# A fused attention and MLP kernel on one core: wider unread matmuls at the start, 256-column cuts, and products in two halves

## The chip, the core and the metric

The kernel runs on one core of a Trainium2 chip. The metric is the device time of one execution in microseconds; the median of the timed runs counts. TensorE (matmul and weight load), VectorE, ScalarE, GpSimd and SyncE each execute their own list of instructions in order and wait for each other by semaphores. In the profile they are PE and PEld, DVE, ACT, POOL and SP.

## The reference

Attention with a sliding window of 128 keys and 4 sink keys, for 4 batches, 8 heads, 768 positions and head size 64, then layer norm and an MLP of widths 512, 2048, 512 with a residual:

```python
scores = scale * np.matmul(q, k.transpose(0, 1, 3, 2))
keep = is_sink | in_window
scores = np.where(keep, scores, -1000000000.0)
a = np.exp(scores - np.max(scores, axis=-1, keepdims=True))
a = a / (np.sum(a, axis=-1, keepdims=True) + 1e-09)
x = np.matmul(a, v)            # heads side by side: [4, 768, 512]
...
xn = (x - mu) / np.sqrt(var + 1e-06) * g_ln
ch = np.maximum(xn @ w_ch1, 0.0) @ w_ch2
return (x + ch).astype(np.float32)
```

## The kernel before

The 3072 rows are 24 tiles of 128, in 12 chunks of two tiles. Every chunk goes through attention (scores, exponentials, mask, values), layer norm, a transpose of the normalised rows, the first MLP layer (L1062: 64 matmuls of 256 columns, eight into each of eight PSUM tiles, each tile followed by a Relu, L1073) and the second layer.

The second layer has two forms. In chunks 0 to 2 it is plain (`second`, L1205): for each tile of 128 rows, 16 matmuls of 512 columns add up in one PSUM bank, four to a step of the plan. From chunk 3 on it is a Strassen-like scheme with seven products instead of eight (`second_by_seven`): VectorE makes sums of halves of the hidden layer (L1090, named s1 to s4, each in two halves m = 0 and 1 of the contraction), and `product` issues eight matmuls of 256 columns (L1113), four on half 0 and four on half 1. Product 6 reads s2, product 5 reads s1, product 7 reads s3, product 3 reads s4. ScalarE and VectorE combine the results (L1119, L1123), and the rows are stored. The last chunk has its own order of the seven products (`last_by_seven`).

No instruction is placed by hand. Each step is recorded with `P.op(name, engines and costs, due time, emit, reads, writes)`. A list scheduler (`Plan.run`) takes, engine by engine, the ready step with the lowest due time inside a small window, and gives it its buffers from rings; the resulting order is fixed in the program. So a changed due time, a step cut in two or a changed list of inputs can move steps on all engines, and the buffers that they take.

After the plan is made, the gaps that it leaves on TensorE in the first 18.5 us of planned time are filled with matmuls on a constant tile of ones; nobody reads their result (L1310). Where the planned gap is over 2 us the kernel before puts in 56 small ones, of 32 columns by 32; there is one such gap, ahead of the mask matmuls L770. Other gaps get 256-column ones:

```python
n = int((room - 0.08) / 0.213) if cold else int((room - 0.15) / 0.13) if room > 0.3 else 0
...
sizes = [512] * (n // 2) + [256] * (n % 2) if cold else [256] * n
if cold and room > 2.0:
    sizes = [512] * PAR["junk"][0] + [32] * PAR["junk"][1]
```

L770 preloads the mask's large negative numbers into PSUM for the first three tiles; L686 loads the first q and k, L690 casts them on ScalarE, L698 and L616 transpose them on TensorE, L669 copies them out of PSUM, L790 and L749 make the first scores, L797 their exponentials, L877 the products with the values.

Of the kernel before, what the change touches and what calls it, by code (L numbers as in the profile page):

```python
# [10 lines left out]
ALU = mybir.AluOpType  # L11
# [185 lines left out]
def pe(us):  # L197
    return {"PE": (us, us + Plan.PE_DRAIN)}
# [12 lines left out]
def fix(occ, extra=0.09):  # L211
# [19 lines left out]
NEVER = -1e9  # L231
BIG = 3.3e38

PAR = dict(w2t_pool=0, junk=(0, 56), rs_nb={4: 48.0, 5: 48.0}, v_nb={8: 50.0, 9: 50.0}, last7=1, opool=0, gk=(5, 4), gv=(4, 5), strict=400.0, win=0.4, tr=-8.0, sc=-5.0, sc1=-2.0, av=2.0, blk=-8.0, step=10.0, trx=9.0, by_dma=4, x_by_dma=3,
           w1p=(1.6, 2.6, 2.7, 2.8), pm=3, w2p=(4.5, 4.51, 4.52, 4.53), apart=2, vs0=(2.0, 13.0), by_tile=0, vp=(0.0, 0.1, 2.0, 2.1, 4.55, 4.56), ld1=0.05, t0=0.8, warm=7.9, pm0=-40.0, w1g=17.0, gtt=1.25, seven=3, lead=(0, 0, 0, 2, 4, 9), w2t=-4.0, at7=(0.5, 1.5, 2.5, 3.5, 4.5, 6.5, 7.5))


# [134 lines left out]
def kernel(  # L372
# [12 lines left out]
    nc = tc.nc  # L385
# [8 lines left out]
    NH1 = DH // 128  # L394
# [687 lines left out]
    def second_by_seven(c, T, h1):  # L1082
        sums = {}

        def half(m, i):
            return h1[m].t.rearrange("p (a n) -> p a n", a=4)[:, :, 128 * i:128 * i + 128]

        def add(n, m, d, in0, in1, op, reads):
            b = sums[n, m] = Buf(f"s{n}_{c}{m}", "sb")
            P.op(f"s{n}_{c}{m}", {"DVE": dve(512, 0.64)}, d, lambda e: V.tensor_tensor(b.t, in0(), in1(), op=op),  # L1090
                 reads=reads, writes=[b])

        for m in range(2):
            add(3, m, T - 3.6 + 2 * m, lambda m=m: half(m, 0), lambda m=m: half(m, 1), ALU.subtract, [h1[m]])
        for m in range(2):
            add(1, m, T - 1.2 + m, lambda m=m: half(m, 1), lambda m=m: half(m + 2, 1), ALU.add, [h1[m], h1[m + 2]])
            add(2, m, T - 1.1 + m, lambda m=m: sums[1, m].t, lambda m=m: half(m, 0), ALU.subtract, [h1[m], sums[1, m]])
            add(4, m, T - 0.5 + m, lambda m=m: half(m + 2, 0), lambda m=m: sums[2, m].t, ALU.subtract, [h1[m + 2], sums[2, m]])

        lo, hi = slice(0, 256), slice(256, 512)  # L1100
        left = {1: lambda m: half(m, 0), 2: lambda m: half(m + 2, 0), 4: lambda m: half(m + 2, 1),
                **{p: (lambda m, n=n: sums[n, m].t) for p, n in ((3, 4), (5, 1), (6, 2), (7, 3))}}
        right = {1: lambda m: w2[m][:, :, lo], 2: lambda m: w2[m + 2][:, :, lo], 3: lambda m: w2[m + 2][:, :, hi],
                 4: lambda m: w2t[3][m], 5: lambda m: w2t[0][m], 6: lambda m: w2t[1][m], 7: lambda m: w2t[2][m]}
        needs = {1: h1[0:2], 2: h1[2:4], 4: h1[2:4], 3: [sums[4, 0], sums[4, 1]], 5: [sums[1, 0], sums[1, 1]],
                 6: [sums[2, 0], sums[2, 1]], 7: [sums[3, 0], sums[3, 1]]}
        w_of = {1: Bw2[0:2], 2: Bw2[2:4], 3: Bw2[2:4], 4: [Bw2t[3]], 5: [Bw2t[0]], 6: [Bw2t[1]], 7: [Bw2t[2]]}

        def product(p, bank, d, new=False, after=()):
            def mm(e):  # L1110
                for m in range(2):
                    for a in range(4):
                        nc.tensor.matmul(bank.t[:, 0:256], lhsT=left[p](m)[:, a, :], rhs=right[p](m)[:, a, :],  # L1113
                                         start=new and m + a == 0, stop=m + a == 4, skip_group_check=True)
            P.op(f"P{p}_{c}", pe(0.875), d, mm, reads=[*needs[p], *w_of[p]], after=after,
                 **({"writes": [bank]} if new else {"rw": [bank]}))

        def keep(name, d, bank, out_b, dst):
            return P.op(f"{name}_{c}", {"ACT": act(256), "DVE": dve(256)}, d, lambda e: (  # L1119
                nc.scalar.copy if e == "ACT" else V.tensor_copy)(dst(), bank.t[:, 0:256]), reads=[bank], writes=out_b)  # L1120

        def plus(name, d, bank, out_b, dst, kept):
            return P.op(f"{name}_{c}", {"DVE": dve(256, 1.06)}, d, lambda e: V.tensor_tensor(  # L1123
                dst(), bank.t[:, 0:256], kept.t, op=ALU.add), reads=[bank, kept], writes=out_b)

        t0, t1 = 2 * c, 2 * c + 1
        ot = [Buf(f"ot{t}", "ot") for t in (t0, t1)]
        oo = [[Buf(f"oo{t}{n}") for n in range(2)] for t in (t0, t1)]
        b0, b1, b2 = (Buf(f"b{n}_{c}", "one") for n in range(3))
        k1, k6, k5 = (Buf(f"{n}_{c}", "tx") for n in ("k1", "k6", "k5"))  # L1130
        at = PAR["at7"]
        if c == NC - 1:
            return last_by_seven(t0, t1, ot, oo, (b0, b1, b2, Buf(f"b3_{c}", "one"), Buf(f"b4_{c}", "one")),
                                 (k1, k6, k5, Buf(f"k12_{c}", "tx")), product, T)
        product(1, b0, T + at[0], True)
        o1 = keep("k1", T - 8, b0, [k1], lambda: k1.t)
        product(7, b2, T + at[1], True)
        product(6, b0, T + at[2], after=[o1])
        o6 = keep("k6", T - 8, b0, [k6], lambda: k6.t)
        product(2, b1, T + at[3], True)  # L1140
        plus("o11", T + at[3], b1, [ot[0], oo[0][0]], lambda: ot[0].t[:, lo], k1)
        product(5, b0, T + at[4], after=[o6])
        o5 = keep("k5", T - 8, b0, [k5], lambda: k5.t)
        o22 = plus("o22", T + at[4], b2, [ot[1], oo[1][0]], lambda: ot[1].t[:, hi], k5)
        product(3, b0, T + at[5], after=[o5])
        keep("o12", T + at[5], b0, [ot[0], oo[0][1]], lambda: ot[0].t[:, hi])
        product(4, b2, T + at[6], after=[o22])
        plus("o21", T + at[6], b2, [ot[1], oo[1][1]], lambda: ot[1].t[:, lo], k6)
        for i, t in enumerate((t0, t1)):
            b, r, x = t // RB, t % RB, x_b[t]  # L1150
            done = Buf(f"of{t}")
            tail["sum", t] = P.op(f"o{t}", {"POOL": (1.1, 1.2)} if PAR["opool"] else {"POOL": (1.1, 1.2), "DVE": dve(512, 1.06)}, T + 9 + i, lambda e, i=i, x=x: (
                V if e == "DVE" else G).tensor_tensor(ot[i].t, ot[i].t, x.t, op=ALU.add), reads=[ot[i], *oo[i], x], writes=[done])  # L1153
            P.op(f"st{t}", {"SP": (0.54, 0.59)}, T + 9.1 + i, lambda e, i=i, b=b, r=r: nc.sync.dma_start(
                out[b, 128 * r:128 * (r + 1), :], ot[i].t), reads=[ot[i], done], dma=HW_S)
# [36 lines left out]
    def second(c, T, h1):  # L1192
        for i in range(2):
# [4 lines left out]
            for f in range(len(cuts) - 1):  # L1198
                pc, wd = Buf(f"pc{t}{f}", "one"), cuts[f + 1] - cuts[f]
                sl = slice(cuts[f], cuts[f + 1])  # L1200
                for s in range(4):
                    def mm(e, s=s, i=i, pc=pc, sl=sl, wd=wd):
                        for ii in range(4):
                            ht = 4 * s + ii
                            nc.tensor.matmul(pc.t[:, 0:wd],  # L1205
                                             lhsT=h1[s].t[:, 256 * ii + 128 * i:256 * ii + 128 * i + 128],
                                             rhs=w2[s][:, ii, sl], start=ht == 0, stop=ht == NH1 - 1)
                    P.op(f"pc{t}{f}_{s}", pe(0.865 * wd / DM), T + 4 * i + s + 4 * f + 0.5, mm,
                         reads=[h1[s], Bw2[s]], **({"writes": [pc]} if s == 0 else {"rw": [pc]}))
                oo = Buf(f"oo{t}{f}")  # L1210
# [74 lines left out]
    for o in order:  # L1285
# [6 lines left out]
        if n > 0:  # L1292
            free = [(max([e_ for b_, e_ in banks[i].lives if b_ < t], default=0.0), i) for i in range(8)
                    if all(e_ < t or b_ > o.start + 0.3 for b_, e_ in banks[i].lives)]
            if free:
                i = min(free)[1]
                sizes = [512] * (n // 2) + [256] * (n % 2) if cold else [256] * n
                if cold and room > 2.0:
                    sizes = [512] * PAR["junk"][0] + [32] * PAR["junk"][1]
                items.append((t + 0.001, -1, (sizes, pairs[i // 2][:, i % 2, :] if i < 4 else ones[i - 4])))  # L1300
        t = o.start + occ * (2 if cold and not o.name.startswith("pm") else 1)
    items.sort(key=lambda z: (z[0], z[1]))
# [2 lines left out]
    with tc.manual_schedule():  # L1305
        for _, s, o in items:
            if s < 0:
                for n in o[0]:
                    m = min(n, 128)
                    nc.tensor.matmul(o[1][0:m, 0:n], lhsT=junk[:, 0:m], rhs=junk[:, 0:n], start=True, stop=True)  # L1310
            elif o is not order_last:
                o.emit(o.eng)
        bad = nc.values_load(flag, min_val=0, max_val=128 * NT * H)
        order_last.emit(order_last.eng)
# [40 lines left out]
```

## Time and profile before

| | |
|---|---|
| timed runs | 209.23, 209.27, 211.8 us; median 209.27 |
| profiled execution | 211.47 us, of which the span of its instructions is 210.0 us |
| TensorE | busy 202.7 us, 97% of the span, 2957 matmuls |
| VectorE, ScalarE, GpSimd | busy 158.8, 122.6 and 116.4 us |
| chain that ended last | TensorE 88%, of the span: L1062 39%, L1113 25%, L1205 10% |

A row of a timeline or chain gives the start in us, the length in us, the engine, the line in the kernel, the operation, the tiles it writes and reads, the shape, and how many instructions were put together (x8). A bracket at its end is the idle time of the engine before it and what ended it. A matmul's own length contains the time to drain, so eight back to back are best read from the start of one group to the start of the next. The windows view gives for a stretch its length, the busy time with the number of instructions, the granted clock of TensorE as a share, the busy share of the DMA engines and the GB/s.

### The profile page before, as it was taken

The page shows a single profiled execution, that of the slowest core. Times are in us where ns is not written, and L with a number is a line of the kernel's source. Part 1 is how long each engine was busy: PE and PEld are TensorE (multiplying, and loading weights), DVE is VectorE, ACT ScalarE, POOL GpSimd, SP SyncE. Part 2 cuts the span into 40 slices and gives each one's busy share as a digit, 9 for nine tenths or more (in the row PEclk, how much of TensorE's full clock was granted, in tenths as well). Part 3 has the DMA queues.
Part 4 walks back from the last instruction along what each step waited for, and adds up shares of the span by engine and source line. Part 5 has one row for each costly group of instructions (what it writes and reads, how often), then busy time and mean ns, then how long its engine had stood idle before and what let it go on. Part 6 is the DMA issues. An engine that isn't in the chain of part 4 may idle for free.

```text
span 210.0 us, 7199 instructions
## 1 busy us (share of the span) xinstructions
PE 202.7 (97%) x2957; PEld 165.3 (79%) x2957; DVE 158.8 (76%) x427; ACT 122.6 (58%) x217; POOL 116.4 (55%) x170
## 2 busy tenths in 40 slices
PE   6799999999999999999999999999999999999992
PEld 4467885674784788888888888888888888888881
DVE  5579885699997678879688688778778778673472
ACT  3668776437495476386485665665664764453610
POOL 7958682479498868937856792793732102410000
PEclk9769999999999999999999999999999999999999
DMA  5999999999999999999999999999995220240202
GB/s 151 192 185 204 187 206 203 166 177 119 149 184 119 150 147 148 111 217 118 107 212 105 101 162 155 106 171 155 107 177 85 78 75 3 77 78 0 103 25 84
DMA packets 104557, 27.82 MB, mean 132 GB/s; under 512 B 93764, under 2 KB 101576, under 8 KB 104520
## 3 DMA queue, kind: packets, MB, share of 16 engines
q0 software_dynamic: 70960, 13.18, 92.7%
q1 hardware_dynamic: 32360, 13.35, 37.6%
q10 hardware_dynamic: 1200, 0.79, 1.3%
q8 instruction: 24, 0.39, 0.8%
q14 instruction: 13, 0.11, 0.3%
HBM read 27.43 MB, written 6.29 MB: 161 GB/s over the span
## 4 chain that ended last, share of the span: by engine, by line
PE 88%; DMA 5%; DVE 3%; ACT 1%; POOL 1%; issue 0%; ACTq 0%; POOLq 0%
PE one L1062 39%; PE one L1113 25%; PE one L1205 10%; DMA natf<-in_q_dram 3%; PE pair L1003 3%; DMA xnt<-xc 2%; PE one L976 2%; PE one L983 1%; PE one L992 1%; PE one L877 1%; PE one L616 1%; PE pair L1011 1%; DVE sb L1090 1%; DVE st L900 1%; PE one L922 1%; PE pair L770 1%
## 5 line engine op out<-in xcount | busy, mean ns | idle before, releaser
L1062 PE MATMUL one<-xnt,w 128*128 128x256 bf16 x768 | 88.7, 273 | 0.2 <-DMA xnt<-xc 0.2
L1062 PEld LDWEIGHTS <-w 128*128 128x128 bf16 x768 | 74.2, 98 | 9.9 <-DMA xnt<-xc 0.4
L1073 ACT ACTIVATE h<-one 128x512 bf16<-128x512 f32 x92 | 54.7, 599 | 35.4 <-PE one L1062 33.9
L664 POOL DMA_DIRECT2D vn<-in_v_dram x59 | 39.1, 684 | 7.8 <-DMA w<-in_moe_w_ch_dram 6.2
L910 POOL TENSOR_SCALAR st<-st 128x1 f32<-128x1 f32 x24 | 9.3, 389 | 50.9 <-DVE st L902 50.6
L1021 ACT ACTIVATE pe<-pair 128x768 bf16<-128x768 f32 x36 | 27.2, 809 | 12.4 <-PE pair L1003 12.4
L1113 PEld LDWEIGHTS <-h 128*128 128x128 bf16 x216 | 20.7, 98 | 2.7
L1205 PE MATMUL one<-w,h 128*128 128x512 bf16 x96 | 22.4, 379 | 0.0
L1119 ACT COPY tx<-one 128x256 f32<-128x256 f32 x24 | 8.9, 372 | 18.2 <-PE one L1113 18.2
L1113 PE MATMUL one<-w,h 128*128 128x256 bf16 x144 | 18.7, 273 | 0.0
L1113 PEld LDWEIGHTS <-sb 128*128 128x128 bf16 x176 | 16.7, 98 | 2.2
L911 POOL TENSOR_TENSOR st<-st,mhalf 128x1 f32<-128x1 f32 x24 | 17.2, 718 | 2.0
L900 DVE BATCH_NORM_STATS2 st<-x 128x6 f32<-128x512 bf16 x24 | 16.6, 694 | 0.8
L1205 PEld LDWEIGHTS <-h 128*128 128x128 bf16 x96 | 9.1, 98 | 9.3
L1046 DVE TENSOR_TENSOR x<-one,rec 128x256 bf16<-128x256 f32 x36 | 15.3, 424 | 1.2
L722 POOL DMA_DIRECT2D nat<-in_k_dram x16 | 15.0, 938 | 1.4 <-DMA natp<-in_q_dram 1.4
L1153 DVE TENSOR_TENSOR ot<-ot,x 128x512 f32<-128x512 f32 x15 | 10.4, 692 | 6.6 <-ACT ot L1119 6.3
L722 POOL DMA_DIRECT2D nat<-in_q_dram x16 | 14.4, 911 | 0.0
L914 DVE TENSOR_SCALAR xc<-x,st 128x512 bf16<-128x512 bf16 x18 | 7.4, 413 | 7.7 <-POOL st L911 7.7
L1113 PE MATMUL one<-natf,sb 128*128 128x256 bf16 x88 | 12.5, 273 | 0.0
L1026 DVE TENSOR_TENSOR pe<-pe,band 128x768 bf16<-128x768 bf16 x24 | 11.9, 539 | 0.0
L1113 PEld LDWEIGHTS <-natc 128*128 128x128 bf16 x112 | 10.9, 98 | 1.3
(148 smaller groups left out, 303.5 us busy)
## 6 DMA issues: line engine op xcount, KB each, us to landing
out_dram<-ot SPq DMA_DIRECT2D x22, 256.0 KB
w<-in_moe_w_ch_dram POOLq DMA_DIRECT2D x6, 512.0 KB, 12.2
nat<-in_k_dram POOLq DMA_DIRECT2D x16, 128.0 KB, 4.7
nat<-in_q_dram POOLq DMA_DIRECT2D x16, 128.0 KB, 6.6
vn<-in_v_dram POOLq DMA_DIRECT2D x44, 32.0 KB, 5.0
w<-in_moe_w_ch_dram POOLq DMA_DIRECT2D x4, 256.0 KB, 11.9
vn<-in_v_dram POOLq DMA_DIRECT2D x15, 64.0 KB, 4.9
natp<-in_k_dram POOLq DMA_DIRECT2D x3, 256.0 KB, 11.2
```

Source lines behind the costliest of these rows:

```text
L664: P.op(f"vld{t}_{i}", {"POOL": (0.8, 0.85)}, prio + 0.001 * i, lambda e, p0=p0, n=n, hs=hs, src=src: G.dma_start(m.t[p0:p0 + n, hs, 0:64], ...
L722: lambda e, nat=nat, ap=ap: G.dma_start(nat.t, ap), writes=[nat], dma=SW_N, after=gate(c))
L900: P.op(f"bn{t}", {"DVE": fix(0.60)}, d + 0.12, lambda e: V.bn_stats(st.t[:, 8:14], x.t), reads=[x], writes=[st, mv])
L911: G.tensor_tensor(st.t[:, 16:17], st.t[:, 17:18], mhalf, op=ALU.pow)),
L1021: nc.scalar.activation(pes[j].t.rearrange("p a b -> p (a b)")[:, 0:768].rearrange("p (a b) -> p a b", a=2), pps[j].t[:, :, 0:384], AF.Exp, ...
L1026: V.tensor_mul(at_s, at_s, band[j] if r > 1 else edge[r][j].unsqueeze(1).to_broadcast([128, 4, 192]))
L1046: P.op(f"x{t - 1}{u}", {"DVE": dve(256)}, d + 0.051 + 0.002 * u, lambda e, u=u, rc=rc, pv=pv: V.tensor_tensor(x.t[:, 256 * u:256 * u + 256 ...
L1062: nc.tensor.matmul(ph.t[:, 256 * s:256 * s + 256], lhsT=w1[ht // 4][:, j, 128 * (ht % 4):128 * (ht % 4 + 1)], rhs=xnt.t[:, j, :], start=j ...
L1073: nc.scalar.activation(dst, ph.t, AF.Relu)
L1113: nc.tensor.matmul(bank.t[:, 0:256], lhsT=left[p](m)[:, a, :], rhs=right[p](m)[:, a, :], start=new and m + a == 0, stop=m + a == 4, skip_g ...
L1153: V if e == "DVE" else G).tensor_tensor(ot[i].t, ot[i].t, x.t, op=ALU.add), reads=[ot[i], *oo[i], x], writes=[done])
L1205: nc.tensor.matmul(pc.t[:, 0:wd], lhsT=h1[s].t[:, 256 * ii + 128 * i:256 * ii + 128 * i + 128], rhs=w2[s][:, ii, sl], start=ht == 0, stop= ...
```

## The change

Four edits.

The rule for the long gap goes: all early gaps are filled by the general rule, and the unread matmuls use all 128 columns of weights. The 56 of 32x32 become five of 512 columns and one of 256. In chunks 1 and 2 (`cut=(1, 2)`) each 512-column matmul of L1205 becomes two of 256 columns with the same weights, into the two halves of the same bank. Each product of the seven becomes two steps of four matmuls, due one after the other, and each half needs only the sums of its own half. The fourth sums of both halves get a later due time, T + 0.9 and T + 1.0 instead of T - 0.5 and T + 0.5.

```diff
-PAR = dict(w2t_pool=0, junk=(0, 56), ...
+PAR = dict(s4=0.9, w2t_pool=0, cut=(1, 2), ...
...
-            add(4, m, T - 0.5 + m, lambda m=m: half(m + 2, 0), lambda m=m: sums[2, m].t, ALU.subtract, [h1[m + 2], sums[2, m]])
+            add(4, m, T + PAR["s4"] + 0.1 * m, lambda m=m: half(m + 2, 0), lambda m=m: sums[2, m].t, ALU.subtract, [h1[m + 2], sums[2, m]])
...
         def product(p, bank, d, new=False, after=()):
-            def mm(e):
-                for m in range(2):
+            for m in range(2):
+                def mm(e, m=m):
                     for a in range(4):
                         nc.tensor.matmul(bank.t[:, 0:256], lhsT=left[p](m)[:, a, :], rhs=right[p](m)[:, a, :],
                                          start=new and m + a == 0, stop=m + a == 4, skip_group_check=True)
-            P.op(f"P{p}_{c}", pe(0.875), d, mm, reads=[*needs[p], *w_of[p]], after=after,
-                 **({"writes": [bank]} if new else {"rw": [bank]}))
+                first = new and m == 0
+                P.op(f"P{p}_{c}{m}", pe(0.4375), d + 0.01 * m, mm, reads=[needs[p][m], *w_of[p]], after=after,
+                     **({"writes": [bank]} if first else {"rw": [bank]}))
...
-                            nc.tensor.matmul(pc.t[:, 0:wd],
-                                             lhsT=h1[s].t[:, 256 * ii + 128 * i:256 * ii + 128 * i + 128],
-                                             rhs=w2[s][:, ii, sl], start=ht == 0, stop=ht == NH1 - 1)
+                            n_cut = 2 if c in PAR["cut"] else 1
+                            for u in range(n_cut):
+                                part = slice(u * wd // n_cut, (u + 1) * wd // n_cut)
+                                nc.tensor.matmul(pc.t[:, part],
+                                                 lhsT=h1[s].t[:, 256 * ii + 128 * i:256 * ii + 128 * i + 128],
+                                                 rhs=w2[s][:, ii, sl.start + part.start:sl.start + part.stop],
+                                                 start=ht == 0 and u == 0, stop=ht == NH1 - 1, skip_group_check=n_cut > 1)
...
-                if cold and room > 2.0:
-                    sizes = [512] * PAR["junk"][0] + [32] * PAR["junk"][1]
...
-                    m = min(n, 128)
-                    nc.tensor.matmul(o[1][0:m, 0:n], lhsT=junk[:, 0:m], rhs=junk[:, 0:n], start=True, stop=True)
+                    nc.tensor.matmul(o[1][:, 0:n], lhsT=junk[:, 0:128], rhs=junk[:, 0:n], start=True, stop=True)
```

More of the change, by code (lines that the diff above doesn't have):

```diff
@@ L232 @@
 BIG = 3.3e38
-PAR = dict(w2t_pool=0, junk=(0, 56), rs_nb={4: 48.0, 5: 48.0}, v_nb={8: 50.0, 9: 50.0}, last7=1, opool=0, gk=(5, 4), gv=(4, 5), strict=400.0, win=0.4, tr=-8.0, sc=-5.0, sc1=-2.0, av=2.0, blk=-8.0, step=10.0, trx=9.0, by_dma=4, x_by_dma=3,
+PAR = dict(s4=0.9, w2t_pool=0, cut=(1, 2), rs_nb={4: 48.0, 5: 48.0}, v_nb={8: 50.0, 9: 50.0}, last7=1, opool=0, gk=(5, 4), gv=(4, 5), strict=400.0, win=0.4, tr=-8.0, sc=-5.0, sc1=-2.0, av=2.0, blk=-8.0, step=10.0, trx=9.0, by_dma=4, x_by_dma=3,
            w1p=(1.6, 2.6, 2.7, 2.8), pm=3, w2p=(4.5, 4.51, 4.52, 4.53), apart=2, vs0=(2.0, 13.0), by_tile=0, vp=(0.0, 0.1, 2.0, 2.1, 4.55, 4.56), ld1=0.05, t0=0.8, warm=7.9, pm0=-40.0, w1g=17.0, gtt=1.25, seven=3, lead=(0, 0, 0, 2, 4, 9), w2t=-4.0, at7=(0.5, 1.5, 2.5, 3.5, 4.5, 6.5, 7.5))
```

## The prediction

> **What bounds the kernel now.** I read the page first, then TensorE's own waits, then its busy time and clock by stretch, and last the order of time in the first 20 us.
>
> ```profile
> span 210.0 us, 7199 instructions
> PE 202.7 (97%) x2957; PEld 165.3 (79%) x2957; DVE 158.8 (76%) x427; ACT 122.6 (58%) x217; POOL 116.4 (55%) x170
> PEclk9769999999999999999999999999999999999999
> PE 88%; DMA 5%; DVE 3%; ACT 1%; POOL 1%; issue 0%; ACTq 0%; POOLq 0%
> ```
>
> TensorE is busy for 97% of the span and holds 88% of the chain that ended last. The clock line has its low digits in the second and third slice only, from about 5 to 15 us. Among the waits of TensorE's matmuls (in all, times, longest) one row belongs to the time after the first stage:
>
> ```profile
> PE one L1062 <- DMA xnt<-xc: 0.2, 1, 0.2
> ```
>
> The windows (busy time, instructions, granted clock, DMA) say the same:
>
> ```profile
> 1.20:4.30 3.10, 3.08 (x60) 1.00 0.60 158
> 4.30:7.70 3.40, 1.91 (x17) 1.00 1.48 245
> 7.70:11.10 3.40, 3.17 (x37) 0.51 2.05 171
> 11.10:14.50 3.40, 3.40 (x41) 0.50 1.57 190
> 14.50:18.00 3.50, 3.30 (x88) 0.99 1.66 189
> 22.00:84.00 62.00, 61.99 (x943) 1.00 1.74 163
> 86.00:205.00 119.00, 119.00 (x1703) 1.00 1.14 109
> ```
>
> From 22 to 205 us, but for that wait near 85, there is no idle TensorE and the clock is full. There, a change counts only by TensorE work added or removed, or by a new wait. Ahead of it are four stretches of about 3.4 us. In the second, TensorE worked 1.91 of 3.40 us; after it the clock was halved for two stretches. The last change to 1.00 follows a stretch that was full, 3.40 of 3.40. The view's 1.00 before 4.3 us is not to be believed; the order of time shows why:
>
> ```profile
> 1.22 1.67 PE L1310 MATMUL pair<-const-bfloat16-1.0 128*32 128x32 bf16 x56 [1.22 <-PEq L1336]
> 2.82 1.76 PE L770 MATMUL pair<-neg,ident 128*128 128x512 bf16 x4
> 4.41 0.27 PE L1310 MATMUL one<-const-bfloat16-1.0 128*128 128x256 bf16 x1
> 5.49 0.40 PE L698 MATMUL one<-ident,natc 128*128 128x128 bf16 x4 [0.81 <-ACT natc L690]
> 7.82 0.61 PE L698 MATMUL one<-ident,natc 128*128 128x128 bf16 x4 [0.21 <-ACT natc L690]
> 8.36 0.40 PE L790 MATMUL pair<-qT,kT 64*128 64x128 bf16 x4
> ```
>
> Four 512-column matmuls took 1.76 us at 2.82, twice the pace of later ones (below), so the clock was low there; the four of L698 took 0.40 us at 5.49 and 0.61 at 7.82. So it opened near 4.3, closed near 7.7 and opened again near 14.5.
>
> **The change, part by part.** First, the orders of the two programs' instructions: on TensorE they differ in the shape of the unread matmuls, in the cut matmuls, and in one group of eight L1062 matmuls that moves ahead of a block. No product is pulled apart, no mode change added; DMA queues keep their order. On VectorE the fourth sum of the first half stands behind the first and second sum of the second half. On ScalarE one Relu moves ahead of three exponentials.
>
> *The cut.* Chunks 1 and 2 have 2 x 2 x 16 = 64 matmuls of 512 columns; they become 128 of 256, with 64 more weight loads.
>
> ```profile
> 63.34 5.18 PE one L1205 x24
> ...
> 135.03 6.11 PE one L1062 x56
> ...
> L1062 PEld LDWEIGHTS <-w 128*128 128x128 bf16 x768 | 74.2, 98 | 9.9 <-DMA xnt<-xc 0.4
> ```
>
> One of 512 costs 5.18/24 = 216 ns, one of 256 with its own load 6.11/56 = 109 ns. So 64 x (2 x 109.1 - 215.8) = 64 x 2.4 ns = +0.15 us, all on the path. A 98 ns load lies inside a 109 ns matmul. If none of the new loads were hidden it would be 64 x 98 ns = +6.3 us. I take +0.15, as the L1062 row is the same shape and the same alternation of load and matmul.
> [...]
>
> *The halves and the later fourth sum.* The eight matmuls of a product stay together, so its TensorE time stays. What could change is a wait. In chunk 7 the sums (VectorE) and products (TensorE) stand so:
>
> ```profile
> 140.98 0.42 DVE L1090 TENSOR_TENSOR sb<-h,sb 128x512 bf16<-128x512 bf16 x1
> 142.27 0.42 DVE L1090 TENSOR_TENSOR sb<-natc,h 128x512 bf16<-128x512 bf16 x1
> 142.73 0.42 DVE L1090 TENSOR_TENSOR natc<-h,sb 128x512 bf16<-128x512 bf16 x1
> 143.66 1.04 PE L1113 MATMUL one<-natf,sb 128*128 128x256 bf16 x8
> 147.16 0.60 PE L1113 MATMUL one<-w,sb 128*128 128x256 bf16 x4
> ```
>
> The rows are the fourth sum of half 0, the second and fourth sum of half 1, product 6 and the first half of product 3. The first row moves behind the second, so the two fourth sums end at 143.15 and, one row of 0.46 us later, at 143.6. Product 3, their reader, starts at 147.16: 3.5 us of cover. The second sums come no later, so product 6 (143.66) finds them as before. What VectorE has queued behind the sums is late by the same 0.46 us, and TensorE waits for none of it today. With the cover gone, two sums would cost 0.9 us. I take 0; bounds -0.2 (the one 0.2 us wait goes) and +0.9 (one such wait). The moved L1062 group and Relu have full neighbours and get 0 within these bounds.
>
> *The wide matmuls, directly.* 56 small ones (1.22 to 2.82) go; five of 512 columns and one of 256 come. At the low clock one of 512 takes 0.43 us (11.98 row below: two in 0.85). So 5 x 0.43 + 0.21 = 2.36: L770 starts at 3.58, not 2.82, 0.76 late. Its four end at 5.30 with the clock low, and the 256 of 4.41 at 5.51; L698 starts at 5.49, when ScalarE delivers. If the clock opens at 4.3 as before, they end at 4.9. Nothing reads L770's result before the scores at 8.36. I take 0; with no cover it is +0.76.
>
> *The wide matmuls, by the clock.* This is the largest term. These rows of the chain ran at half clock, followed by two of the same kind after the opening:
>
> ```profile
> 7.82 0.62 PE one L698 x4
> ...
> 9.60 0.82 PE pair L790 x12
> 10.43 1.00 PE one L616 x16
> 11.42 0.55 PE one L877 x8
> 11.98 0.85 PE pair L770 x2
> 12.83 0.54 PE pair L790 x8
> 13.37 0.54 PE pair L1310 x2
> 13.91 0.89 PE one L616 x16
> 14.80 0.54 PE pair L770 x2
> 15.34 0.26 PE one L877 x8
> ```
>
> The eight low rows hold 5.81 us. Halved they would save 2.9; by rows with a partner, L770 saves 0.31 of 0.85, L877 0.29 of 0.55, L698 0.21 of 0.61, or 0.81 of 2.01. At that 40% the eight save 2.3. ScalarE and VectorE lie between, so 0 is the other end. The runs speak for the upper end: the profiled execution took 211.47 us (210.0 and 1.47 around it), two of three timed runs 209.23 and 209.27, the third 211.8. The 2.2 us between are about what an open clock saves, so I read the two as runs in which it did not close; no trace of them shows it. After the change the stretch 4.3 to 7.7 gets about 0.4 us more work (up to 4.9 instead of 4.5): 1.91 becomes 2.3 of 3.4. That is toward open, not surely enough: 3.30 of 3.50 kept it open. I take -2.2 against the profiled execution; bounds -2.9 and 0.
> [...] The stretches between the trace's clock changes agree in length, 6.8 us for two. [...]
>
> **Sum.** 211.47 + 0.15 + 0 + 0 - 2.2 = 209.4 us, 0.15 over the median of 209.27. The verdict's bound is 2%, about what a measurement of this kernel can tell from no change: faster is under 205.1, slower over 213.5.
>
> **The rivals.**
> - *The clock closes in most runs:* 211.47 + 0.15 = 211.6. For it: the profiled execution, and 2.3 of 3.4 is still well below full. Against it: two of three runs at 209.2 with less early work.
> - *The clock stays low longer.* The shifted work moves the second opening from 14.5 to 21.4, two stretches; each costs up to half of 3.4 us, so 211.6 + 3.4 = 215.0, slower. It decides if the stretch 11.1 to 14.5 fails to open the clock. For it: 3.17 of 3.40 us did not open it before. Against it: no instruction after 7.7 changes in the first stage.
> - *The new weight loads show:* 209.27 + 6.3 = 215.6, slower, from the first cut chunk on. Against it stand the 768 matmuls of L1062 and 504 of L1113 that hide them. [...]
> - *The wide matmuls hold up the transposes* (the change fills no idle time but takes time): 209.4 + 0.76 = 210.2. Against it: L698 waits for ScalarE until 5.49.
> - *More is won at the start:* the 209.2 us runs still had one low stretch; half of the 2.3 comes off: 208.2. TensorE work from 22 us on leaves no way under 205.1.
>
> **How the numbers follow.** Forecast 0.55; clock closed 0.25; low longer 0.07; weight loads 0.03; transposes held up 0.04; more at the start 0.03; of 0.03 left, 0.01 is slower (the 0.9 us wait in each of nine chunks), 0.02 faster. So slower 0.11, faster 0.02, within 2% 0.87. The range 208.0 to 212.2 takes in the forecast with its +0.9 and -0.2, the closed case with +0.6, the gain at the start and the held-up case, some 0.85 in all.
>
> **What would show it.** After: L1310 as five of 512 and one of 256 from 1.2 to about 3.6; L770 from about 3.6; L698 still ended by ScalarE near 5.5. Clock 1.00 in 7.7 to 14.5 and the first L1062 2 us earlier if the clock term is right; 0.5 there and an outcome near 211.6 if the closed rival is. L1205's 256-column matmuls at 109 ns each, 48 in about 5.24 us where 24 took 5.18. Product 3 without a wait. The forecast is wrong if TensorE shows idle time of over 1 us between 22 and 205, or steps of over 200 ns in the cut matmuls.

## The result, and the profile after

The changed kernel took 211.6 us (median of 20 runs, 210.88 to 214.7), the kernel before 209.7 us (20 runs, 209.17 to 211.83). The ratio is 1.0071, 95% interval 1.0042 to 1.0101: within 2%, as forecast, inside the range of 208.0 to 212.2, but on its slow side and not at 209.4. Its profiled execution took 210.88 us, its span is 209.3 us.

The rows of the page that answer to those of before, then TensorE's windows (length, busy time with instructions, granted clock, DMA share, GB/s):

```profile
span 209.3 us, 7227 instructions
PE 201.4 (96%) x2971; PEld 169.5 (81%) x2971; DVE 157.7 (75%) x427; ACT 122.6 (59%) x217; POOL 116.4 (56%) x170
PEclk9999999999999999999999999999999999999999
PE 77%; DVE 8%; DMA 8%; POOL 2%; ACT 1%; issue 1%; ACTq 0%; POOLq 0%; DVEq 0%
```

```profile
1.20:4.30 3.10, 3.08 (x8) 1.00 0.54 157
4.30:7.70 3.40, 2.74 (x19) 1.00 1.48 247
7.70:11.10 3.40, 2.79 (x49) 1.00 2.06 172
11.10:14.50 3.40, 3.40 (x71) 1.00 1.59 188
22.00:84.00 62.00, 61.15 (x981) 1.00 1.73 166
86.00:205.00 119.00, 118.87 (x1701) 1.00 1.09 108
```

Two things changed. The clock row has no low digit any more: the two stretches from 7.7 to 14.5 us, at 0.51 and 0.50 before, are at 1.00. And the body, full before, has gaps: 61.15 of 62.00 us and 118.87 of 119.00. TensorE's share of the chain falls from 88% to 77%; DMA and VectorE take it over, each at 8%. TensorE's waits name the place, and its order of time shows the start and the gaps:

```profile
PE pair L1011 <- DMA qT<-nat: 0.6, 1, 0.6
PE one L1062 <- DMA xnt<-xc: 0.5, 1, 0.5
```

```profile
1.22 2.52 PE L1312 MATMUL pair<-const-bfloat16-1.0 128*128 128x512 bf16 x6 [1.22 <-PEq L1338]
3.53 1.91 PE L770 MATMUL pair<-neg,ident 128*128 128x512 bf16 x4
5.50 0.51 PE L698 MATMUL one<-ident,natc 128*128 128x128 bf16 x4
...
17.25 0.94 PE L1062 MATMUL one<-xnt,w 128*128 128x256 bf16 x6
...
58.99 0.30 PE L1011 MATMUL pair<-qT,kts 128*32 128x128 bf16 x8 [0.61 <-DMA qT<-nat]
...
84.25 0.94 PE L1062 MATMUL one<-xnt,w 128*128 128x256 bf16 x7 [0.49 <-DMA xnt<-xc]
```

The chain of waits has the cut matmuls of chunk 2:

```profile
62.01 5.24 PE one L1209 x48
```

A good way to follow the time is the start of the same TensorE group in both traces. The changed kernel's first L1062 starts at 17.25 us, the other's at 19.54: a lead of 2.29 us. At 37 us it is 2.14, at 54 us 2.02, behind the wait at 58 us 1.32, at 80 us 1.24, behind the wait at 84 us 0.92, and behind a step of 0.29 us at 101 us 0.63. That stays to the end: spans of 209.3 and 210.0. So 1.66 us of a 2.29 us gain were given back: 0.20 to the cut itself, 0.14 at 30 us, and 0.70, 0.32 and 0.29 us net to the three waits. This execution, 210.88 us, is the shortest of the 20; what the median of 211.6 has beyond it is in no trace.

### The profile page after: what moved, and what is told of

It is laid out like the page before. It is cut to its first block, busy times and chain, and to the rows that moved or that the text cites. A ratio compares the mean times of both kernels' runs of the same rounds, so it can differ in the third digit from the quotient of the medians.

```text
span 209.3 us, 7227 instructions
## 1 busy us (share of the span) xinstructions
PE 201.4 (96%) x2971; PEld 169.5 (81%) x2971; DVE 157.7 (75%) x427; ACT 122.6 (59%) x217; POOL 116.4 (56%) x170
## 4 chain that ended last, share of the span: by engine, by line
PE 77%; DVE 8%; DMA 8%; POOL 2%; ACT 1%; issue 1%; ACTq 0%; POOLq 0%; DVEq 0%
PE one L1062 35%; PE one L1113 22%; PE one L1209 10%; DMA qT<-nat 3%; DMA natf<-in_q_dram 3%; DMA xnt<-xc 2%; PE pair L1003 2%; DVE sb L1090 2%; DVE st L900 2%; PE one L976 1%; PE one L983 1%; DVE x L1046 1%; POOL st L911 1%; PE one L992 1%; PE pair L1011 1%
## 5 line engine op out<-in xcount | busy, mean ns | idle before, releaser
L1062 PE MATMUL one<-xnt,w 128*128 128x256 bf16 x768 | 88.8, 273 | 0.5 <-DMA xnt<-xc 0.5
L1062 PEld LDWEIGHTS <-w 128*128 128x128 bf16 x768 | 74.2, 98 | 10.1 <-DMA xnt<-xc 0.8
L1113 PEld LDWEIGHTS <-h 128*128 128x128 bf16 x216 | 20.7, 98 | 3.1 <-issue 0.3
L1209 PE MATMUL one<-w,h 128*128 128x256 bf16 (+1 forms) x160 | 22.6, 294 | 0.0
L1209 PEld LDWEIGHTS <-h 128*128 128x128 bf16 x160 | 15.2, 98 | 4.7 <-DMA w<-in_moe_w_ch_dram 0.3
```

Source lines behind the costliest of these rows:

```text
L1062: nc.tensor.matmul(ph.t[:, 256 * s:256 * s + 256], lhsT=w1[ht // 4][:, j, 128 * (ht % 4):128 * (ht % 4 + 1)], rhs=xnt.t[:, j, :], start=j ...
L1209: nc.tensor.matmul(pc.t[:, part], lhsT=h1[s].t[:, 256 * ii + 128 * i:256 * ii + 128 * i + 128], rhs=w2[s][:, ii, sl.start + part.start:sl. ...
```

## The experiments

Each ratio is taken against runs of the kernel before made beside the experiment. The median of that kernel was 209.7 us beside the change and 210.65 to 211.63 us beside the experiments, so medians of different experiments are not compared with each other. Its shortest run was 209.1 to 209.3 us each time, so shortest runs can be.

Each timed run also gives a mean granted clock. In the traces it is 0.977 to 0.984 where the clock closed again near 8 us, and 0.996 or more elsewhere. Runs of 0.99 and less are counted as closed below; runs of 0.991 to 0.993 lie between the two, and no trace shows one. The mean doesn't mark a late first opening, since the time ahead of the first change is counted as full (the halves' execution below opened at 14.03 us and shows 0.997). So times of "0.995 and more" hold early and late openings, and an early lead is read from traces alone.

**The wide unread matmuls alone.** The kernel before with the change's two hunks on the unread matmuls; the rule taken out is

```diff
-                if cold and room > 2.0:
-                    sizes = [512] * PAR["junk"][0] + [32] * PAR["junk"][1]
```

> The wide unread matmuls alone; everything else as before. Theory A (the gain at the start is real and is taken back by transfers that do not come earlier): clock 1.00 in the stretch 7.7 to 14.5 us, first L1062 near 17.3 us instead of 19.5, but new TensorE waits of 1 to 2 us in all between 50 and 105 us, most of them for the DMA transposes of q and x; time 210.5 to 211.6. Theory B (the loss lies in the new order that halves and cut bring): same start, waits under 0.5 us, time 208.5 to 209.3, and all runs close together.

212.71 us, 6 runs, 1.0105 (1.0054 to 1.0155): longer than either theory expected. The profiled execution, 211.06 us, is the shortest of the six. It won 2.22 us at the start and had 0.36 us of it left at 61 us:

```profile
PE pair L1003 <- DMA qT<-nat: 1.2, 1, 1.2
PE pair L1011 <- DMA qT<-nat: 0.3, 1, 0.3
```

By group starts these took 1.35 and 0.39 us of the lead, as theory A has it. So a gain at the start is not kept by itself: chunk 4's two transposes of q left SyncE 0.6 and 1.1 us earlier than in the profile of before (at 52.45 and 53.78 instead of 53.04 and 54.87), while TensorE came for them 2.10 us earlier. The other five runs took 212.24 to 213.37 us at a mean clock of 0.991 to 0.993, and what makes them longer still is in no trace.

**The cut alone.** L1205 as in the change, nothing else.

> The 256-column cut of chunks 1 and 2 alone. Both theories: +0.15 us on TensorE, 24 matmuls of 5.18 us become 48 of 5.24. Theory A: start and spread as before, 209.5 to 212, no new wait. Theory B gives up to +1 us more if the cut is what makes new waits.

211.49 us, 12 runs, 1.0056 (1.0015 to 1.0097), lowest 210.47. So the cut alone does make a new wait, as theory B allowed. There is none at 58 us, but this one:

```profile
84.57 0.61 PE L1062 MATMUL one<-xnt,w 128*128 128x256 bf16 x4 [1.44 <-DVE ot L1123]
```

The view names VectorE, the last event that it saw. VectorE had been done long before; what came last were the transposed rows xnt (1.60 us by group starts; the lead falls from 1.88 to 0.59, since the kernel before waits 0.3 us here). SyncE's queue tells why, read together with the DMA issues: the second k load of chunk 6 was issued at 72.06 and landed at 78.08, 6.0 us later.

```profile
75.54 3.74 SPq L595 DMA_TRANSPOSE kT<-nat  x2
79.37 1.22 SPq L595 DMA_TRANSPOSE xnt<-xc  x1
```

The second of the two k transposes waited for that load until 78.09; the rows, which VectorE had ready at 77.85, stood behind it in the in-order queue and left at 79.37.

**The halves and the later fourth sum alone.**

> Products in two halves and the later fourth sum alone. Theory A: as before within 0.3 us, 209.3 to 212 with the same spread as before. Theory B: a wait of product 4 on the combination L1124 in chunk 4 of 0.3 us or more and others behind late VectorE work; 1 to 2 us slower than before at the same clock.

210.1 us, 12 runs, 0.9981 (0.9947 to 1.0016): no difference. Their trace has a step of 0.30 us at 101.3, where product 4 waits for the combination L1124 on VectorE; the 0.3 us wait of before near 85 is gone. In this trace they cancel.

**Cut and halves with the 56 narrow matmuls**, that is the changed kernel without its wide ones.

> The changed kernel with the 56 small unread matmuls put back (cut, halves and later fourth sum stay). Theory A: the clock closes in part of the runs as before, TensorE waits in the body nearly gone in those runs; 209.4 to 212, like before. Theory B: 211 to 212, as slow as the changed kernel or slower, since the start is worse too.

212.94 us, 12 runs, 1.0085 (1.0041 to 1.013), longer than either theory expected. Its trace has waits of 1.33 us at 82.8 and 0.90 us at 99.3, both of L1062 for transposed rows; the lead of 2.27 us is used up by 100 us. So without the wide matmuls the change loses no less in its trace (2.27 us) than with them (1.66), only later.

**Two further executions of the kernel before.** The kernel is the same.

> The kernel before once more, for a trace of a shorter execution (its runs lie between 209.2 and 212.6 us). Theory A (a lead won at the start is taken back where TensorE meets DMA transposes): in an execution with an open clock from 7 us on, TensorE is 2.3 us ahead at the first L1062, and the eighth-chunk work at 85 us starts no earlier than 84.2; total near 211. Theory C (transfers can follow the lead, and the other edits keep them from it): in such an execution the group that stood at 85.17 starts near 82.9, TensorE waits under 0.4 us between 20 and 205, total 209.2.

> The same kernel, a second look. Theory A and theory C as for the first look. If the clock opens first at 14 us, both say: first L1062 about 0.25 us before that of the first trace, total 211.

209.37 and 209.28 us. The clock opened at 9.32 and 5.25 us and stayed open. The first L1062 starts 1.94 and 2.49 us earlier than in the profile of before, and at the end 2.08 and 2.16 us are left. TensorE's windows of the second:

```profile
4.30:7.70 3.40, 2.20 (x19) 1.00 1.50 244
7.70:11.10 3.40, 2.92 (x53) 1.00 2.05 173
11.10:14.50 3.40, 3.40 (x70) 1.00 1.59 188
```

So the kernel before reaches the open clock by itself, and its transfers can follow a lead of 2 us, as theory C has it. At 58 us its L1011 starts straight behind L1003:

```profile
57.76 0.52 PE L1003 MATMUL pair<-qT,kT 64*64 64x128 bf16 x32
58.21 0.29 PE L1011 MATMUL pair<-qT,kts 128*32 128x128 bf16 x8
```

**The changed kernel with small stores.** In chunks 0 to 2 it stores 8 rows of each tile instead of 128; the other rows are left out.

> The changed kernel, with the six output stores of chunks 0 to 2 cut from 128 rows to 8 (the other rows of these tiles are not written); the order of all instructions is the changed kernel's. Theory A: 1.4 MB fewer in the stretch 35 to 75 us brings the transposes of q, k and x earlier, the waits of 0.77 us near 58 and 0.65 us near 84 fall under 0.3 each; 210.0 to 210.8 against 211.6. If the waits hang on the order of VectorE and GpSimd work and not on DMA traffic: both waits stay within 0.2 us, 211.3 to 211.9.

210.8 us, 10 runs, 1.0012 (0.9967 to 1.0058). The wait at 58 us is gone from its trace, a wait of 0.60 us near 84 and the step of 0.29 at 101 remain. But waits of 0.50 us at 17.7 and 0.34 at 46.3 had cut its lead to 1.14 us at 54 us, where the changed kernel had 2.02; TensorE came for the transposes of q 0.9 us later, so that the missing wait doesn't show that the stores' traffic made it. Only this is shown: the wait near 84 us doesn't need those stores.

**One exchange in SyncE's queue.** A single line behind the plan sends tile 9's rows ahead of chunk 6's second k transpose; all other engines' lists stay the same.

```diff
-    order = P.run()
+    order = P.run(); by = {o.name: o for o in order}; by["trk61"].start = by["trx9"].start + 1e-4; order.sort(key=lambda o: (o.start, o.seq))
```

> The cut alone, with two neighbours of SyncE's queue exchanged: the transpose of tile 9's normalised rows (xnt<-xc) goes ahead of the second k transpose of chunk 6 (kT<-nat); every other engine's list stays as in the cut alone. Theory Q (head of the queue): in the cut alone the k load landed at 78.08, the k transpose in front waited for it, and the rows, ready at 77.85, were sent at 79.37; first-layer group M32 then waited 1.6 us. With the exchange the rows go out near 77.9, M32 waits 0 to 0.3 us, and the runs at an open clock fall from 210.5-211.2 to 209.2-209.8. Rival T (traffic): the landing is slow because the transfer engines are full; the rows go out earlier but land no earlier, M32 still waits over 1 us, and the open-clock runs stay at 210.5 and more.

In the cut: 211.21 us, 12 runs, 1.0004 (0.9972 to 1.0036). Its four runs at a clock of 0.995 and more took 209.42, 209.87, 210.0 and 210.08, all below the lowest of the cut without the exchange (210.47). Theory Q holds in direction, a little short in size: 209.2 to 209.8 was expected. Its one trace fell on an execution whose clock closed, so it can't show the wait of 84 us with a lead; that trace has a wait of 1.0 us for rows at 101 us.

> The changed kernel with the same exchange on SyncE's queue. Theory Q: of its new waits the 0.65 us at 83.5 goes, the 0.77 us at 58 and the 0.29 us at 101 stay; 0.4 to 0.6 us less than the changed kernel, so a ratio near 1.0045 and runs near 211.0. Rival T: no difference from the changed kernel, 1.0071.

In the changed kernel: 211.37 us, 12 runs, 1.0016 (0.9981 to 1.0051), lowest 209.62, where the changed kernel's lowest is 210.88. How much it gains is unclear. The ratio falls from 1.0071 to 1.0016, some 1.2 us and more than the 0.4 to 0.6 expected, but the two intervals overlap, and the medians themselves differ by 0.2 us alone. In its trace the rows left SyncE at 78.43 instead of 79.77 and landed at 82.44 instead of 84.21, and the wait of 0.65 us at 84 is gone. But the transposes of q make TensorE wait twice.

```profile
PE pair L1011 <- DMA qT<-nat: 1.6, 2, 1.1
```

These are 0.65 us at 58 us and 1.28 us at 75 us by group starts. Both come before the exchanged steps leave SyncE, so the exchange didn't make them; the second one is not in the changed kernel's trace, and by it the lead was down to 0.04 us ahead of 84. So this trace shows that the rows land earlier, not what that is worth with a lead.

> The kernel before with the same exchange. If its own runs of 210.4 to 211.5 us at an open clock come from the same meeting on SyncE's queue, they fall to 209.2-209.6 and the median goes to 209.5 at most, ratio near 0.995. If they come from the transposes of q near 58 us or from elsewhere, the two groups of runs stay and the ratio is 1.000.

In the kernel before: 209.51 us, 12 runs, 0.9956 (0.9918 to 0.9994), the best version of this study. Seven of its 12 runs are at 209.2 to 209.6 and five still at 210.9 to 212.5. Its trace opened at 6.66 us, keeps a lead of 2.24 us to the end, and its queue is as meant:

```profile
75.04 1.19 SPq L595 DMA_TRANSPOSE kT<-nat  x1
77.65 1.19 SPq L595 DMA_TRANSPOSE xnt<-xc  x1
78.93 1.22 SPq L595 DMA_TRANSPOSE kT<-nat  x1
```

None of its 12 runs had the closed clock, of the kernel before 8 of 35 beside it, so part of the 0.4% may be that. A gain of this size is not proven by an interval that ends at 0.9994. And the two groups of runs stay, so the meeting on SyncE's queue is not all that divides them.

**The cut's 0.15 us without the cut.**

```diff
-                            nc.tensor.matmul(pc.t[:, 0:wd],
...
+                            for wn in ([176] if ht == 0 and i == 0 and c in (1, 2) else []) + [wd]:
+                                nc.tensor.matmul(pc.t[:, 0:wn], ...
```

> The kernel before with 0.15 us of TensorE work put in where the cut has its 0.15 us, without the cut: one matmul of 176 columns in chunk 1 and one in chunk 2, whose result the next matmul overwrites. Theory S (the shift is the cause): the same late transfers as with the cut alone, open-clock runs at 210.5 to 211.2 and none at 209.2-209.5, ratio 1.004 to 1.006. Rival C (something in the cut itself): +0.15 us, ratio 1.0007, and open-clock runs near 209.4 remain.

210.36 us, 12 runs, 0.9983 (0.994 to 1.0026). Five of its eight runs at 0.995 and more took 209.34 to 209.52; the cut has none below 210.47. So rival C holds: being 0.15 us later is not what costs the cut its 1.2 us (0.56%), something else that comes with the cut is.

**Fewer unread matmuls.** The kernel before with `sizes = [256] * 6` in the long gap: as many instructions as the wide version, as short as the narrow one.

> The kernel before with six unread matmuls of 256 columns in the first gap in place of 56 of 32 by 32: as many instructions on TensorE as with the wide ones alone (100 fewer than before), but about as short as the 56 (6 x 0.21 us, so L770 near 2.5 us, not 3.5). [...]

213.61 us, 6 runs, 1.0126 (1.0064 to 1.0187), all at 212.97 and more. The run was to tell two causes apart for the waits near 58 us of the wide version: the place of the 16 KB packets on the queue that the DMA view names `q8 instruction`, or the wide matmuls' own time or shape. It doesn't decide. In two of the six runs the clock closed, which the wide ones never showed. The profiled execution fell on a closed clock, without a lead and so without a wait at 58 us. What made it long was the end: from the last store's issue to the end of the span it took 5.78 us (206.72 to 212.50), in the other thirteen traces 3.4 to 3.5. In the trace's instructions TensorE's last branch stands out:

```
few:    207.58 3.80 Tensor COMPARE_BRANCH L1315
wide:   206.93 0.51 Tensor COMPARE_BRANCH L1312
before: 207.35 0.41 Tensor COMPARE_BRANCH L1315
```

While it runs, so does a 16 KB packet of the queue q8, from 208.57 to 209.96 us. The trace has 24 such packets (0.39 MB) for some 5800 instructions of TensorE, about 240 for each, and the branch took 3.4 us more than in the kernel before; of that, 2.3 us show in the span. That the packet held the branch up is not shown: in the trace of before such a packet runs at the end, too, from 208.49 to 209.80 us, behind a branch of 0.41 us. If the four runs at 0.995 and more had this end too, which no trace shows, 2.3 off leaves 210.7 to 211.7, which either an early clock with the wait at 58 or a late one without it would give.

## Why the prediction was right, and where it was wrong

*The cut, +0.15.* Right for TensorE. The 48 of chunk 2 took 5.24 us, the number forecast; over both chunks the lead lost 0.20. The rival that weight loads show (+6.3) falls: 48 matmuls of 109 ns fill the 5.24 us and leave no room for 48 loads of 98 ns. But "+0.15, all on the path" was not the cut's price: alone it made the kernel 0.56% slower, some 1.2 us, through a transfer.

*The halves and the later sum, 0 with +0.9 at most.* Right: 0.9981 (0.9947 to 1.0016). Product 3 found its sums; 0.3 us appeared at product 4's wait for a combination on VectorE, which the prediction had not named.

*The wide matmuls, directly.* Right: L770 at 3.53 (3.58 forecast), L698 at 5.50 (5.49), no loss.

*The wide matmuls, by the clock, -2.2.* Right in size: the first L1062 came 2.29 us earlier. None of the 48 runs of the four kernels with the wide ones has a mean clock of 0.99 or less, 37 of the 160 of the seven kernels with the 56 narrow ones do; so the wide ones do keep the clock from closing near 8 us. (Six of the 48 and eight of the 160 are at 0.991 to 0.993, which stays open.) How they do it is not shown. The prediction had the clock open at 4.3 us and filled the stretch behind that; in the trace it opened at 5.78, and in no trace with the wide ones before 5.46. Over all 14 traces, all four openings at 4.3 to 4.9 us were followed by a closing 3.4 us later, none of the ten later ones was. So the edit mends about one run in five, and the median of before was one of the others; the prediction had this from two of three runs at 209.2, and the two further executions confirm that such runs have the open clock.

*The step that failed* is the row of the body: "There, a change counts only by TensorE work added or removed, or by a new wait", and then no new wait was priced for it. The sum carried the 2.2 us won at 17 us unchanged through to 205 us. The missing term is the waits for transposes at 58 and 84 us and the step at 101, 1.3 us in this trace and 1.7 in that of the wide ones alone. With 1.3 added, 209.4 becomes 210.7, near the profiled 210.88; the 0.7 us from there to the median is not explained. The prediction's own test for this was idle time over 1 us between 22 and 205; it occurred, so the forecast of 209.4 was wrong by that test. That the time fell into the range is luck: the range reached to 212.2 for a closed clock, and the outcome equals the closed-clock rival's 211.6 by number, not by mechanism.

An early start alone doesn't make these waits. In the profile of before the second transpose of q for chunk 4 left SyncE at 54.87 us and landed at 59.79, only 0.52 us ahead of its use; yet the first of the two further executions kept its lead, because there the transpose left 2.51 us and landed 2.09 us earlier. In the changed kernel it left earlier still and was longer on the way:

```profile
52.23 6.71 DMA qT<-nat
```

That is 6.71 us from leaving to landing, against 4.92 in the profile of before and 5.34 in that execution.

*What made the transfers late.* Shown: in the cut, SyncE's queue held ready rows behind a transpose that waited for a load (with the exchange, its shortest run falls from 210.47 to 209.42 us). Not shown: why that load is late in the cut, and why the transposes of q are longer on the way with the wide matmuls than in the kernel before. One thing fits, the 16 KB packets of the queue q8. The cut adds 128 TensorE instructions, the wide version takes away 100, the shift adds 4, and the packets stand at other times in these traces (below); that the one makes the other was not shown. The DMA queues of the changed kernel's trace from 53 to 55.5 us, when the transposes of q are under way (packets, MB, share of 16 engines):

```profile
q8 instruction: 1, 0.02, 4.2%
```

The packet starts at 53.41 us and takes 1.67. The wide version has one in this stretch, too, with 4.1%; in the kernel before with the open clock and in the cut alone the stretch has no such packet (49.98 and 59.3 in the first), and they have no wait at 58. In the cut one lies at 75.01 us, inside the late k load of 72.06 to 78.08; in the kernel before it comes at 77.31, after the load's landing at 75.88. With small stores the packet is at 54.01 and no wait follows, though the lead there was only 1.14. Over all 14 traces, the second transpose of q took 5.8 to 6.7 us in the five where such a packet starts while it is under way, 4.3 to 5.8 in the nine others. For the k load it is less clear: 4.2 to 6.1 us in seven traces with a packet, 4.3 to 5.6 in seven without. A packet and a late transfer can have a common cause, so this is not proof. The run meant to settle it, with few unread matmuls, didn't; it stays open.

## What to carry to other kernels

A full TensorE in one trace says that the others kept up with that start, not that they keep up with an earlier one: before carrying a gain at the start through to the end, look for each transfer how long before its use it landed. Where this cover is less than the gain, ask whether the transfer will leave earlier by as much and take no longer, and price a wait if that isn't sure. In a queue that is worked off in order, as SyncE's is in these traces (rows ready at 77.85 us left at 79.37), look at what stands behind a step that waits for a load. And where a kernel shows two levels of time, take several traces of it before one of them is used as the base of a sum.

## What the runs showed of the hardware that was not expected

- In one trace of 14 TensorE's last branch took 3.80 us instead of 0.4 to 0.5, with a 16 KB packet of the queue q8 running meanwhile (208.57 to 209.96 us), and the span ended 2.3 us later. The kernel had 100 instructions fewer than before; the wide version has as few and did not pay that in its trace, so the number alone doesn't decide it.
- In these 14 traces the clock's fate early in the kernel went with when it first opened: at 4.32, 4.44, 4.63 and 4.84 us it closed again 3.41 us later and stayed low for 6.83; at 5.25 us and later (ten traces) it stayed.
- A 128 KB load on the software queue took 4.3 and 6.0 us from issue to landing at the same place of nearly the same program (the kernel before, 71.56 to 75.88; the cut, 72.06 to 78.08).
